# Head-slot DMAs moved from SyncE to GpSimd, with smaller gate/up weight buffers

## The chip, the cores and the metric

The kernel runs on one core of a Trainium2 chip. The metric is the device time of one launch in microseconds. The profile is one execution of the same program, recorded by the hardware profiler.

## The reference

Inputs are bf16: x [1, 2048, 576], wqkv [576, 1728], wo [576, 576], w_gate and w_up [576, 4608], w_down [4608, 576].

```python
def attention(xn):                      # 32 heads of 18, causal, window 256
    q, k, v = split_heads(xn @ wqkv)
    scores = (q @ k.T) * 18 ** -0.5
    p = softmax(where(0 <= i - j < 256, scores, -1e9))
    return merge_heads(p @ v) @ wo

def gated_ffn(xn):
    return (sigmoid(xn @ w_gate) * (xn @ w_up)) @ w_down

xn = layernorm(x)                       # no scale, no shift
out = x + attention(xn) * silu(gated_ffn(xn))
```

## The kernel before, in words

The 2048 rows are handled in four chunks of 512 (four blocks of 128). Each chunk goes through these steps: the layer norm (`build_ln`, L359), which leaves the transposed chunk in `xnT` (TensorE transposes at L394); the V projection (L469, L472); the q/k projection (`build_qk`, L408); attention for eight head groups of four heads (`build_attn`, L494); the output projection (`build_wo`, L593); and the FFN (`build_ffn`, L644). The FFN's first product makes gate and up for 36 tiles of 128 columns (L687, and L697 for the last 64 rows of the contraction). Its second product contracts over these 36 tiles (L743, L745).

**The head slots.** The q/k projection makes 1152 columns in nine tiles of 128, two tiles to a group, so five groups. VectorE copies a group from PSUM to `qd` (L430). A head has 18 columns, and the score product wants each head at a partition that is a multiple of 32, so for each head's q and each head's k one DMA inside SBUF moves its 18 rows of 512 bf16 elements into its slot in `qT` or `kT`. A head that straddles two tiles takes two DMAs. That gives 72 DMAs per chunk and 288 in all: 16 in each of the first four groups, 8 in the fifth. A head group's score products (L523) wait for all slot DMAs of the groups that hold its columns: head group 0 needs group 0, head group 1 needs groups 0 and 1, head group 7 needs groups 3 and 4. `qd` has two buffers, `qT` has four.

**The weights.** The gate/up weights are read from HBM again in every chunk, because SBUF doesn't hold them. `wgs` has two buffers, each for four of the 36 tiles; `weights(fg)` (L659) fills one with four DMAs: 512 rows of gate, 64 rows of gate, the same for up. A row of such a transfer is 512 columns, 1024 bytes. A buffer is released by the last product of its four tiles. `w_down` is loaded once, during chunk 0, and stays.

**What sets the order.** Every instruction is an `Op` with an engine, an estimated duration, what it depends on and a priority (0 goes first). `schedule` (L779) simulates the five engines with these estimates and takes, for each engine in turn, the operation with the smallest (start + 150 ns x priority). What comes out is one fixed list per engine, and each engine works through its list in order; nothing is reordered on the chip. All DMAs are issued by SyncE: `dma` (L187) makes an `Op` on "SP" of 620 ns, with 2000 ns to landing and 280 bytes per ns for all of them together. Loads of x have priority 0, slot DMAs 1, `wqkv` and stores 2, gate/up weights 3, `w_down` and the second read of x 6. Compute on the attention side has priority 1, on the FFN side 3, so the FFN fills the gaps of attention.

A DMA carries a semaphore of its own lane, which counts 16 when the transfer has landed; `emit` (L851) puts the waits ahead of the instruction that needs them. GpSimd ("POOL") has only the constants at the start (L316 to L332) and one small operation per block in the layer norm, the power that makes `rstd` (L377). VectorE's next step of the norm (L381) waits for it.

Of the kernel before, what the change touches and what calls it, by code (L numbers as in the profile page):

```python
# [18 lines left out]
BPC = NT // P  # L19
FG = 4  # L20
NFG = NFT // FG
EPS = 1e-5
SM_SCALE = float(DH) ** -0.5

# [9 lines left out]
NFIN = 2  # L34
NQK = 5

DMA_ISSUE_NS = 620.0
DMA_LAT_NS = 2000.0
DMA_BYTES_PER_NS = 280.0

# [118 lines left out]
class Builder:  # L159
# [24 lines left out]
            d.succs.append(o)  # L184
        return o

    def dma(self, dst, src, nbytes, name, lane, deps=(), prio=2):  # L187
        o = self.op("SP", DMA_ISSUE_NS, lambda eng: eng.dma_start(dst, src), name, deps, prio, nbytes=nbytes)  # L188
        o.lane = self.lane_ids.setdefault(lane, len(self.lane_ids))
        return o  # L190

    def alloc_memory(self):
        nc = self.nc
        bf16, f32 = dt.bfloat16, dt.float32
        cur = [(nc.sbuf_base + 63) // 64 * 64]
        top = nc.sbuf_top

        def size(shape, dtp):
            n = 1
            for s_ in shape[1:]:  # L200
                n *= s_
            return n * mybir.dt.size(dtp)

        def seq(name, shape, dtp=bf16):
            off = cur[0]
            cur[0] = (off + size(shape, dtp) + 31) // 32 * 32
            assert cur[0] <= top, f"out of SBUF at {name}: {cur[0]} > {top}"
            return nc.alloc_sbuf_tensor_at(name, list(shape), dtp, offset=off), off

        self.xnT, _ = seq("xnT", [P, 2, KT, NT])  # L210
        self.wd_sb, _ = seq("wd_sb", [P, NFT, D])
        self.hT, _ = seq("hT", [P, NFT, NT])
        self.wgs, _ = seq("wgs", [P, 2, 9, FG * P])
        self.tring, _ = seq("tring", [P, 2, NT])
        self.v_aug, _ = seq("v_aug", [P, NVB, H, DH + 1])
        self.qT, _ = seq("qT", [P, NQS, NT])
        self.kT, _ = seq("kT", [P, 2, NHG, NT])
        self.expr, zex = seq("expr", [P, NEX, 4, NT])
        self.stage = nc.alloc_sbuf_tensor_at("stage", [P, KT, 2 * D], bf16, offset=zex)
        assert size([P, KT, 2 * D], bf16) <= size([P, NEX, 4, NT], bf16)  # L220
        self.o_tok, _ = seq("o_tok", [P, BPC * D + 64])
        self.oT, _ = seq("oT", [P, 2, KT, P])
        self.s_attn, _ = seq("s_attn", [P, 2 * BPC, D])
        self.wqk, _ = seq("wqk", [P, KT, 2 * D])
        self.wv_sb, _ = seq("wv_sb", [P, KT, D])
        self.wo_sb, _ = seq("wo_sb", [P, KT, D])
        self.qd, _ = seq("qd", [P, NQD, 2, NT])
        self.xr, _ = seq("xr", [P, NXR, D])
        self.xnr, _ = seq("xnr", [P, NXN, KT * P])
        self.xf, _ = seq("xf", [P, NFIN, D])  # L230
        self.thf, _ = seq("thf", [P, NFIN, D])
        self.ident, _ = seq("ident", [P, P])
        self.mask, _ = seq("mask", [P, 4, P])
        self.neghalf, _ = seq("neghalf", [P, 1], f32)
        self.bnst, _ = seq("bnst", [P, NST, 2, 6], f32)
        self.mv, _ = seq("mv", [P, NST, 2], f32)
        self.veps, _ = seq("veps", [P, NST, 1], f32)
        self.rstd, _ = seq("rstd", [P, NST, 1], f32)
        self.rrec, _ = seq("rrec", [P, 2, 4 * BPC], f32)
        if self.verbose:  # L240
            print(f"SBUF used up to {cur[0]} of {top} ({top - cur[0]} free)")
        self.ps = nc.alloc_psum_tensor("ps", [P, 4096], f32)
        self.psb = self.ps.bitcast(bf16)
        self.pool_s = Pool("S", [0, 1])
        self.pool_f = Pool("F", [2, 3])

    def build_graph(self):
        self.r_xr = Ring(NXR, "xr")
        self.r_xn = Ring(NXN, "xnr")
        self.r_st = Ring(NST, "stats")  # L250
        self.r_qd = Ring(NQD, "qd")
        self.r_q = Ring(NQS, "q")
        self.r_ex = Ring(NEX, "expr")
        self.r_rec = Ring(2, "rrec")
        self.r_oT = Ring(2, "oT")
        self.r_w = Ring(2, "wgs")
        self.r_t = Ring(2, "tring")
        self.r_xf = Ring(NFIN, "xf")
        self.r_th = Ring(NFIN, "th")
        self.xnT_rel = [[] for _ in range(NC)]  # L260
        self.op_xnT = [[] for _ in range(NC)]
        self.op_v = {}
        self.op_vis = {}
        self.last_vis = None
        self.ffn_last = None
        self.op_pv = {}
        self.op_on = {}
        self.op_s = {}
        self.op_q2 = {}
        self.otr_last = []  # L270
        self.prev_f2_last = None
        self.x_dma = {}
        self.q_slot = {}
        self.op_sp = {}
        self.sp_grp = {}
        self.hg_grps = {}

        self.load_x(0)
        self.build_consts()
        for c in range(NC):  # L280
            self.build_ln(c)
            self.build_v(c)
            made = 0
            for hg in range(NHG):
                need = min(NQK, (8 * UNIT * (hg + 2) - 1) // (2 * P) + 1)
                while made < need:
                    self.build_qk(c, made)
                    made += 1
                self.build_attn(c, hg)
            self.build_wo(c)  # L290
            self.build_ffn(c)
# [116 lines left out]
    def build_qk(self, c, gi):  # L408
# [25 lines left out]
        for j in range(NUNIT):  # L434
            hg, w, h4 = j // 8, (j % 8) // 4, j % 4
            for i, t in enumerate(ts):
# [9 lines left out]
                else:  # L446
# [1 line left out]
                    dst = self.kT[p0:p0 + hi - lo, par, hg, :]  # L448
                src = self.qd[lo - t * P:hi - t * P, sq, i, :]
                o = self.dma(dst, src, (hi - lo) * NT * 2, f"dma:sp:{c}:{j}:{t}", ("qk", par, gi),  # L450
                             deps=[ev, war], prio=1)
                self.op_sp.setdefault((c, hg), []).append(o)
                self.sp_grp.setdefault((c, gi), []).append(o)
                self.r_qd.release(sq, o)
# [189 lines left out]
    def build_ffn(self, c):  # L644
# [11 lines left out]
            self.ffn_last = o  # L656
            return o

        def weights(fg):  # L659
            sw, dw = self.r_w.produce()  # L660
            fc = slice(fg * FG * P, (fg + 1) * FG * P)
            ds = []
            for w, (src, nm) in enumerate(((self.wg, "g"), (self.wu, "u"))):
                ds.append(self.dma(self.wgs[:, sw, 4 * w:4 * w + 4, :],
                                   src[0:512, fc].rearrange("(kt p) f -> p kt f", p=P), 512 * 512 * 2,
                                   f"dma:w{nm}:{c}:{fg}", ("w", sw, w), deps=[dw], prio=3))
                ds.append(self.dma(self.wgs[64 * w:64 * w + 64, sw, 8, :], src[512:576, fc], 64 * 512 * 2,
                                   f"dma:w{nm}4:{c}:{fg}", ("w", sw, 2 + w), deps=[dw], prio=3))
            slots[fg] = sw
            wops[fg] = ds  # L670
            if c == 0:
                self.op_wd.append(self.dma(
                    self.wd_sb[:, fg * FG:(fg + 1) * FG, :],
                    self.wd[fg * 512:(fg + 1) * 512, :].rearrange("(kt p) d -> p kt d", p=P), 512 * D * 2,
                    f"dma:wd{fg}", ("wd", fg), deps=[hm.get(fg * FG - FG)], prio=6))

        def bank(h, w):
            o = h.units[0] * 1024 + 512 * w
            return self.ps[:, o:o + 512]

        def main(ft, h, w, first, acq):
            sw, fc = slots[ft // FG], slice((ft % FG) * P, (ft % FG + 1) * P)

            def f(eng):
                res = None
# [1 line left out]
                    res = eng.matmul(bank(h, w), self.wgs[:, sw, 4 * w + kt, fc], x_in[:, kt, :],  # L687
                                     start=(first and kt == 0), stop=(not first and kt == 3))
                return res
            return pe(4 * mm_ns(NT), f, f"f1{'gu'[w]}:{c}:{ft}", [self.op_xnT[c], wops[ft // FG]], acq)  # L690

        def rem(eng, ft, h, first):
            sw, fc = slots[ft // FG], slice((ft % FG) * P, (ft % FG + 1) * P)
            res = None
            for w in range(2):
                r = slice(64 * w, 64 * w + 64)
                res = eng.matmul(bank(h, w), self.wgs[r, sw, 8, fc], x_in[r, 4, :], start=first, stop=not first,  # L697
                                 tile_position=(64 * w, 0))
            return res
# [12 lines left out]

        for fa in range(0, NFT, 2):
            fb = fa + 1
            if fa % FG == 0:
                weights(fa // FG)
            ha, hb = self.pool_f.hold(), self.pool_f.hold()
            main(fa, ha, 0, True, ha)
            main(fa, ha, 1, True, None)
# [6 lines left out]
            g = main(fb, hb, 0, False, None)  # L726
            u = main(fb, hb, 1, False, None)
            tail(fb, hb, g, u)
            if fb % FG == FG - 1:
                self.r_w.release(slots[fb // FG], u)  # L730
        self.xnT_rel[c].append(self.ffn_last)

        new_last = [None] * NFG
# [45 lines left out]
    def schedule(self):  # L779
# [13 lines left out]
        while nsched < len(ops):  # L793
# [32 lines left out]
            if o.acq is not None:  # L826
                o.deps += [d for d in o.acq.pool.take(o.acq, units) if d not in o.deps]
            o.start = stt
            if o.eng == "SP":
                free["SP"] = stt + o.est  # L830
                o.end = max(stt + o.est + DMA_LAT_NS, bw_clock + o.nbytes / DMA_BYTES_PER_NS)
                bw_clock = max(bw_clock, stt + o.est) + o.nbytes / DMA_BYTES_PER_NS
            else:
# [17 lines left out]
    def emit(self):  # L851
        nc = self.nc
        ENGS = ("PE", "ACT", "DVE", "POOL", "SP")
        for o in self.ops:
            if o.eng == "SP":
                o.needs_tok = True
            for d in o.deps:
                d.needs_tok = True
# [3 lines left out]
        for e in ENGS:  # L862
            for o in self.prog[e]:
                if not o.needs_tok:
                    continue
                if e == "SP":
                    lane_cnt[o.lane] += 16
                    o.tok = (("L", o.lane), lane_cnt[o.lane])
                else:
# [6 lines left out]
        def run_engine(e, eng):  # L876
            known = {}
            for o in self.prog[e]:
# [9 lines left out]
                    eng.wait_ge(semof(k), v)  # L888
                ins = o.fn(eng)
                if o.needs_tok:  # L890
                    ins.then_inc(semof(o.tok[0]), 16 if e == "SP" else 1)
            if e == "SP":
                for i, n in enumerate(lane_cnt):
                    if n > 0:
# [65 lines left out]
```

## Time and profile before

| what | us |
|---|---|
| median of 3 runs | 690.53 |
| lowest and highest run | 689.25, 694.64 |
| the profiled execution | 692.99 |
| its span, first to last instruction | 691.3 |
| mean granted TensorE clock in it | 0.958 of 2.4 GHz |

The rows below are from the profiled execution. Engines are PE (TensorE's matmuls), PEld (its weight loads), DVE (VectorE), ACT (ScalarE), POOL (GpSimd) and SP (SyncE). A name with q behind it, as SPq, is the engine's queue of instructions; a DMA is issued there, and its issue doesn't count as busy time. L188 is the line in `dma` that issues every DMA. A tile is named as the program names it: `wgs<-in_B_w_up_dram` is a load of up weights, `qT<-qd` a slot DMA. Times are in us from the start of the span, unless a column says ns.

### The profile page before, as it was taken

The page shows a single profiled execution, that of the slowest core. Times are in us where ns is not written, and L with a number is a line of the kernel's source. Part 1 is how long each engine was busy: PE and PEld are TensorE (multiplying, and loading weights), DVE is VectorE, ACT ScalarE, POOL GpSimd, SP SyncE. Part 2 cuts the span into 40 slices and gives each one's busy share as a digit, 9 for nine tenths or more (in the row PEclk, how much of TensorE's full clock was granted, in tenths as well). Part 3 has the DMA queues.
Part 4 walks back from the last instruction along what each step waited for, and adds up shares of the span by engine and source line. Part 5 has one row for each costly group of instructions (what it writes and reads, how often), then busy time and mean ns, then how long its engine had stood idle before and what let it go on. Part 6 is the DMA issues. An engine that isn't in the chain of part 4 may idle for free.

```text
span 691.3 us, 13052 instructions
## 1 busy us (share of the span) xinstructions
PE 615.9 (89%) x5555; PEld 288.5 (42%) x5652; DVE 284.3 (41%) x493; ACT 290.4 (42%) x302; POOL 15.5 (2%) x32
## 2 busy tenths in 40 slices
PE   3997796999889999579959999997899999999996
PEld 1442242444445444224425554443344454333453
DVE  3664353534544643333534324555352222333222
ACT  3444444636446642355656314756452101322200
POOL 4110000000000000000000000000000000000000
PEclk9999898999999999789989999999899999999999
DMA  9515626415011320144052001233323311555000
GB/s 286 167 40 160 199 81 183 141 52 164 11 31 45 95 70 13 51 123 134 15 149 70 19 14 53 86 89 90 120 86 85 123 35 54 155 155 151 2 29 23
DMA packets 64425, 63.08 MB, mean 91 GB/s; under 512 B 5808, under 2 KB 63792, under 8 KB 64368
## 3 DMA queue, kind: packets, MB, share of 16 engines
q1 hardware_dynamic: 64368, 62.25, 30.1%
q8 instruction: 44, 0.72, 0.4%
q14 instruction: 13, 0.11, 0.1%
HBM read 55.15 MB, written 2.36 MB: 83 GB/s over the span
## 4 chain that ended last, share of the span: by engine, by line
PE 72%; SPq 11%; DMA 6%; DVE 4%; issue 3%; ACT 3%; DVEq 0%; ACTq 0%
PE ps L687 32%; PE ps L743 15%; SPq L188 11%; PE ps L564 5%; PE ps L697 4%; PE ps L421 4%; PE ps L523 3%; PE ps L745 3%; DMA wgs<-in_B_w_up_dram 3%; PE ps L627 3%; PE ps L469 2%; ACT expr L539 2%; DMA xr<-in_A_x_dram 1%; DMA wv_sb<-in_A_wqkv_dram 1%; DVE hT L706 1%
## 5 line engine op out<-in xcount | busy, mean ns | idle before, releaser
L687 PE MATMUL ps<-xnT,wgs 128*128 128x512 bf16 x1102 | 276.1, 391 | 31.5 <-DMA wgs<-in_B_w_up_dram 20.4
L539 ACT ACTIVATE expr<-ps 128x2048 bf16<-128x2048 f32 (+1 forms) x96 | 170.0, 1771 | 121.0 <-PE ps L523 120.6
L687 PEld LDWEIGHTS ps<-xnT,wgs 128*128 128x128 bf16 x1152 | 103.2, 99 | 168.7 <-issue 65.2
L743 PE MATMUL ps<-wd_sb,hT 128*128 128x512 bf16 x543 | 143.9, 385 | 0.0
L703 ACT ACTIVATE tring<-ps 128x512 bf16<-128x512 f32 x144 | 84.6, 597 | 139.0 <-PE ps L697 119.0
L547 DVE TENSOR_TENSOR expr<-expr,mask 128x1536 bf16<-128x1536 bf16 (+2 forms) x96 | 78.9, 824 | 150.7 <-ACT expr L539 150.7
L706 DVE SCALAR_TENSOR_TENSOR hT<-tring,ps 128x512 bf16<-128x512 bf16 x144 | 97.6, 685 | 102.4 <-ACT tring L703 70.0
L745 PE MATMUL ps<-wd_sb,hT 128*128 128x64 bf16 x576 | 111.7, 194 | 2.3 <-issue 0.7
L743 PEld LDWEIGHTS ps<-wd_sb,hT 128*128 128x128 bf16 x576 | 56.8, 99 | 69.0 <-issue 5.5
L745 PEld LDWEIGHTS ps<-wd_sb,hT 128*128 128x128 bf16 x576 | 56.8, 99 | 0.5
L523 PE MATMUL ps<-qT,kT 18*128 18x256 bf16 (+1 forms) x960 | 38.1, 251 | 16.0 <-ACT expr L539 8.7
L564 PEld LDWEIGHTS ps<-v_aug,expr 128*128 128x128 bf16 x1440 | 40.5, 96 | 13.3 <-DVE expr L547 4.9
L697 PE MATMUL ps<-xnT,wgs 64*128 64x512 bf16 x288 | 45.7, 398 | 0.0
L421 PE MATMUL ps<-xnT,wqk 128*128 128x512 bf16 x175 | 43.0, 392 | 2.6 <-ACT expr L539 2.4
L564 PE MATMUL ps<-v_aug,expr 128*128 128x19 bf16 x1440 | 41.2, 172 | 4.6 <-DVE expr L547 2.3
L766 ACT ACTIVATE thf<-ps 128x576 bf16<-128x576 f32 x16 | 10.4, 649 | 75.1 <-PE ps L745 75.0
L523 PEld LDWEIGHTS ps<-qT,kT 18*128 18x128 bf16 x960 | 15.9, 93 | 55.8 <-ACT expr L539 21.5
L768 DVE SCALAR_TENSOR_TENSOR thf<-thf,ps 128x576 bf16<-128x576 bf16 x16 | 12.0, 752 | 61.5 <-ACT thf L766 61.5
L430 DVE CAST qd<-ps 128x1024 bf16<-128x1024 f32 (+1 forms) x20 | 22.3, 1117 | 28.1 <-PE ps L421 28.1
L421 PEld LDWEIGHTS ps<-xnT,wqk 128*128 128x128 bf16 x180 | 17.4, 100 | 24.3 <-ACT expr L539 3.6
L469 PE MATMUL ps<-wv_sb,xnT 128*128 128x512 bf16 x73 | 20.3, 406 | 3.1 <-DMA wv_sb<-in_A_wqkv_dram 2.3
L638 ACT ACTIVATE s_attn<-ps 128x576 bf16<-128x576 f32 x16 | 10.4, 650 | 23.3 <-PE ps L630 23.3
(44 smaller groups left out, 209.8 us busy)
## 6 DMA issues: line engine op xcount, KB each, us to landing
wgs<-in_B_w_gate_dram SPq DMA_DIRECT2D x36, 512.0 KB, 4.2
wgs<-in_B_w_up_dram SPq DMA_DIRECT2D x36, 512.0 KB, 5.3
wd_sb<-in_B_w_down_dram SPq DMA_DIRECT2D x9, 576.0 KB, 5.9
wgs<-in_B_w_gate_dram SPq DMA_DIRECT2D x36, 64.0 KB, 4.0
wgs<-in_B_w_up_dram SPq DMA_DIRECT2D x36, 64.0 KB, 4.9
xf<-in_A_x_dram SPq DMA_DIRECT2D x16, 144.0 KB, 2.1
out_dram<-xf SPq DMA_DIRECT2D x16, 144.0 KB, 1.9
qT<-qd SPq DMA_DIRECT2D x112, 18.0 KB
```

What stands on the lines that cost most here:

```text
L188: o = self.op("SP", DMA_ISSUE_NS, lambda eng: eng.dma_start(dst, src), name, deps, prio, nbytes=nbytes)
L421: res = eng.matmul(self.ps[:, b + i * 512:b + (i + 1) * 512], self.wqk[:, kt, t * P:(t + 1) * P], self.xnT[:, xs, kt, :], start=(kt == 0), ...
L523: res = eng.matmul(self.ps[:, o:o + nq * P], self.kT[r, kp, hg, ko:ko + P], self.qT[r, qs, q0 * P:(q0 + nq) * P], start=True, stop=True, t ...
L539: return eng.activation(dst, src, ACTF.Exp, scale=SM_SCALE)
L547: return eng.tensor_tensor(e_, e_, m_, ALU.mult)
L564: res = eng.matmul(self.ps[:, o:o + 19], self.expr[:, se, h4, at * P:(at + 1) * P], self.v_aug[:, kb % NVB, hg * 4 + h4, :], start=(n == 0 ...
L687: res = eng.matmul(bank(h, w), self.wgs[:, sw, 4 * w + kt, fc], x_in[:, kt, :], start=(first and kt == 0), stop=(not first and kt == 3))
L697: res = eng.matmul(bank(h, w), self.wgs[r, sw, 8, fc], x_in[r, 4, :], start=first, stop=not first, tile_position=(64 * w, 0))
L703: th = op("ACT", act_ns(NT), lambda e: e.activation(self.tring[:, st, :], bank(h, 0), ACTF.Tanh, scale=0.5), f"th:{c}:{ft}", deps=[pg, dt_ ...
L706: mu = op("DVE", dve_ns(NT), lambda e: e.scalar_tensor_tensor(self.hT[:, ft, :], self.tring[:, st, :], 1.0, bank(h, 1), ALU.add, ALU.mult) ...
L743: eng.matmul(self.ps[:, b:b + 512], self.hT[:, ft, cols], self.wd_sb[:, ft, 0:512], start=(ft == 0), stop=(ft == NFT - 1))
L745: res = eng.matmul(self.ps[:, b + 512:b + 576], self.hT[:, ft, cols], self.wd_sb[:, ft, 512:576], start=(ft == 0), stop=(ft == NFT - 1))
```

## The change

Slot DMAs are issued from GpSimd's queue, and the planner counts 1000 ns for each there; a DMA on SP counts 600 ns. `wgs` has four buffers of two tiles, in the same memory, so a transfer's row is 256 columns (512 bytes), and each chunk has 18 loads of four DMAs. The first such load of chunk 0 has priority 1, all others 3 as before. `w_down` keeps its loads of four tiles. The rest of the diff lets the planner and `emit` treat a DMA by its lane and not by its engine.

```diff
+WG = 2
+NWS = 4
-DMA_ISSUE_NS = 620.0
+DMA_ISSUE_NS = {"SP": 600.0, "POOL": 1000.0}
...
-    def dma(self, dst, src, nbytes, name, lane, deps=(), prio=2):
-        o = self.op("SP", DMA_ISSUE_NS, lambda eng: eng.dma_start(dst, src), name, deps, prio, nbytes=nbytes)
+    def dma(self, dst, src, nbytes, name, lane, deps=(), prio=2, eng="SP"):
+        o = self.op(eng, DMA_ISSUE_NS[eng], lambda e: e.dma_start(dst, src), name, deps, prio, nbytes=nbytes)
...
-        self.wgs, _ = seq("wgs", [P, 2, 9, FG * P])
+        self.wgs, _ = seq("wgs", [P, NWS, 9, WG * P])
...
-        self.r_w = Ring(2, "wgs")
+        self.r_w = Ring(NWS, "wgs")
...
                 o = self.dma(dst, src, (hi - lo) * NT * 2, f"dma:sp:{c}:{j}:{t}", ("qk", par, gi),
-                             deps=[ev, war], prio=1)
+                             deps=[ev, war], prio=1, eng="POOL")
...
-        def weights(fg):
+        def weights(wg):
             sw, dw = self.r_w.produce()
-            fc = slice(fg * FG * P, (fg + 1) * FG * P)
+            pr = 3 if c or wg else 1
+            fc = slice(wg * WG * P, (wg + 1) * WG * P)
...
-            if fa % FG == 0:
-                weights(fa // FG)
+            if fa % WG == 0:
+                weights(fa // WG)
+            if c == 0 and fa % FG == 0:
+                load_wd(fa // FG)
...
-            if fb % FG == FG - 1:
-                self.r_w.release(slots[fb // FG], u)
+            if fb % WG == WG - 1:
+                self.r_w.release(slots[fb // WG], u)
...
-            if o.eng == "SP":
-                free["SP"] = stt + o.est
+            if o.lane is not None:
+                free[o.eng] = stt + o.est
```

## Rows read from the trace of the kernel before

**Rows 1.** The page, busy time, share of the span and instructions of each engine.

```profile
PE 615.9 (89%) x5555; PEld 288.5 (42%) x5652; DVE 284.3 (41%) x493; ACT 290.4 (42%) x302; POOL 15.5 (2%) x32
```

**Rows 2.** The page, shares of the span in the chain that ended last, by engine.

```profile
PE 72%; SPq 11%; DMA 6%; DVE 4%; issue 3%; ACT 3%; DVEq 0%; ACTq 0%
```

**Rows 3.** The waits of engines and of SP's queue: total us, times, longest us.

```profile
PE ps L687 <- DMA wgs<-in_B_w_up_dram: 20.4, 6, 3.8
...
DVE bnst L369 <- DMA xr<-in_A_x_dram: 13.2, 5, 7.5
...
SPq L188 <- DVE xf L774: 94.9, 10, 25.8
```

**Rows 4.** SP's queue in time, start of chunk 2: start us, us, instruction, count.

```profile
266.60 3.05 SPq L188 DMA_DIRECT2D qT<-qd  x4
...
289.90 0.66 SPq L188 DMA_DIRECT2D kT<-qd  x1
290.60 1.03 SPq L188 DMA_DIRECT2D wgs<-in_B_w_gate_dram  x2
```

**Rows 5.** TensorE in time; in brackets its idle time before, and what ended it.

```profile
13.71 2.29 PE L469 MATMUL ps<-wv_sb,xnT 128*128 128x512 bf16 x5 [2.33 <-DMA wv_sb<-in_A_wqkv_dram]
...
287.84 3.90 PE L421 MATMUL ps<-xnT,wqk 128*128 128x512 bf16 x9 [2.38 <-ACT expr L539]
...
297.70 3.19 PE L687 MATMUL ps<-xnT,wgs 128*128 128x512 bf16 x7 [3.43 <-DMA wgs<-in_B_w_up_dram]
```

**Rows 6.** The chain that ended last, in order of time: start us, us, what.

```profile
192.80 2.65 DMA qT<-qd
...
290.56 0.04 issue
...
292.31 4.88 DMA wgs<-in_B_w_up_dram
...
415.10 1.75 DMA kT<-qd
```

**Rows 7.** Stretches: from:to, length, busy time of each engine, PEclk, DMA share, GB/s.

```profile
0.00:13.70 13.70, 1.98 (x15) 1.37 (x16) 5.87 (x25) 5.27 (x6) 8.08 (x20) 1.00 0.88 275
53.00:82.00 29.00, 21.30 (x179) 7.97 (x182) 10.19 (x17) 12.97 (x14) 0.00 (x0) 0.82 0.63 191
104.00:125.00 21.00, 14.84 (x131) 5.76 (x135) 7.70 (x14) 10.73 (x12) 0.00 (x0) 0.84 0.58 177
162.00:200.00 38.00, 33.36 (x405) 17.88 (x412) 19.00 (x42) 16.61 (x13) 2.29 (x3) 0.91 0.29 85
277.00:318.00 41.00, 27.02 (x266) 11.20 (x269) 14.07 (x20) 19.31 (x17) 0.00 (x0) 0.75 0.35 101
347.00:365.00 18.00, 10.84 (x129) 4.52 (x129) 6.26 (x9) 9.79 (x8) 0.00 (x0) 0.81 0.47 141
474.00:490.00 16.00, 11.23 (x81) 3.90 (x81) 5.08 (x8) 8.10 (x6) 0.00 (x0) 0.79 0.54 159
365.00:474.00 109.00, 105.97 (x1148) 54.04 (x1165) 49.77 (x78) 54.62 (x50) 0.00 (x0) 1.00 0.18 54
577.00:651.00 74.00, 73.63 (x357) 28.86 (x363) 26.43 (x39) 21.95 (x37) 0.00 (x0) 1.00 0.39 116
```

**Rows 8.** Instructions of line 188: count, issue time ns min/median/max, first and last start us.

```profile
L188 SPq DMA_DIRECT2D qT<-qd x144: 560/698/945, 26.0 to 478.2; - x144
L188 SPq DMA_DIRECT2D kT<-qd x144: 557/698/798, 29.2 to 481.1; - x144
L188 SPq DMA_DIRECT2D wgs<-in_B_w_gate_dram x72: 367/517/1971, 5.1 to 634.6; - x72
```

**Rows 9.** Groups of instructions by line: busy us, mean ns | idle before, releaser.

```profile
L377 POOL TENSOR_TENSOR rstd<-veps,neghalf 128x1 f32<-128x1 f32 x16 | 9.6, 607 | 161.0 <-DVE veps L375 161.0
...
L547 DVE TENSOR_TENSOR expr<-expr,mask 128x1536 bf16<-128x1536 bf16 (+2 forms) x96 | 78.9, 824 | 150.7 <-ACT expr L539 150.7
...
L381 DVE TENSOR_SCALAR xnr<-xr,mv,rstd 128x576 bf16<-128x576 bf16 x16 | 6.5, 425 | 3.6 <-POOL rstd L377 3.3 <-PE ps L394 0.3
```

More of the change, by code (lines that the diff above doesn't have):

```diff
@@ L664, in weights, with load_wd @@
                 ds.append(self.dma(self.wgs[:, sw, 4 * w:4 * w + 4, :],
[L665 to L675, printed above, removed]
+                                   src[0:512, fc].rearrange("(kt p) f -> p kt f", p=P), 512 * WG * P * 2,
+                                   f"dma:w{nm}:{c}:{wg}", ("w", sw, w), deps=[dw], prio=pr))
+                ds.append(self.dma(self.wgs[64 * w:64 * w + 64, sw, 8, :], src[512:576, fc], 64 * WG * P * 2,
+                                   f"dma:w{nm}4:{c}:{wg}", ("w", sw, 2 + w), deps=[dw], prio=pr))
+            slots[wg] = sw
+            wops[wg] = ds
+        def load_wd(fg):
+            self.op_wd.append(self.dma(
+                self.wd_sb[:, fg * FG:(fg + 1) * FG, :],
+                self.wd[fg * 512:(fg + 1) * 512, :].rearrange("(kt p) d -> p kt d", p=P), 512 * D * 2,
+                f"dma:wd{fg}", ("wd", fg), deps=[hm.get(fg * FG - FG)], prio=6))
         def bank(h, w):
@@ L681, in main @@
         def main(ft, h, w, first, acq):
-            sw, fc = slots[ft // FG], slice((ft % FG) * P, (ft % FG + 1) * P)
+            sw, fc = slots[ft // WG], slice((ft % WG) * P, (ft % WG + 1) * P)
             def f(eng):
@@ L689, in f @@
                 return res
-            return pe(4 * mm_ns(NT), f, f"f1{'gu'[w]}:{c}:{ft}", [self.op_xnT[c], wops[ft // FG]], acq)
+            return pe(4 * mm_ns(NT), f, f"f1{'gu'[w]}:{c}:{ft}", [self.op_xnT[c], wops[ft // WG]], acq)
         def rem(eng, ft, h, first):
-            sw, fc = slots[ft // FG], slice((ft % FG) * P, (ft % FG + 1) * P)
+            sw, fc = slots[ft // WG], slice((ft % WG) * P, (ft % WG + 1) * P)
             res = None
@@ L854, in emit @@
         for o in self.ops:
-            if o.eng == "SP":
+            if o.lane is not None:
                 o.needs_tok = True
@@ L865, in emit @@
                     continue
-                if e == "SP":
+                if o.lane is not None:
                     lane_cnt[o.lane] += 16
@@ L890, in run_engine @@
                 if o.needs_tok:
-                    ins.then_inc(semof(o.tok[0]), 16 if e == "SP" else 1)
+                    ins.then_inc(semof(o.tok[0]), 16 if o.lane is not None else 1)
             if e == "SP":
```

## The prediction

> **What bounds the kernel now.** I read the page's busy line, its chain, the list of waits, then the SP queue and TensorE side by side in time, and last a table of stretches. TensorE is busy for 615.9 of 691.3 us [rows 1]: it is the bound, and what can be won is its idle time and its time at the lower clock. The chain that ended last is 72% TensorE, but 11% (some 78 us) of it is SP's queue issuing DMAs and 6% is DMA [rows 2]. The waits say what TensorE misses: six stalls on gate/up weights, 20.4 us in all; VectorE loses 13.2 us to late loads of x, 7.5 of them in one wait that a mask multiplication stands behind [rows 3].
>
> Why are weights late? SP's own time line shows it [rows 4]. From 266.60 to 290.56 us SP issues 32 head-slot transfers for chunk 2, the first two of its five groups: 23.96 us, 0.75 us each. The weights that chunk 2's FFN wants are issued behind them, at 290.60. TensorE meanwhile first waits for exponentials with nothing else in its list (2.38 us before 287.84), then 3.43 us for those weights [rows 5], and the chain of that stretch runs along the slot issues into the weight transfer, which takes 4.88 us from 292.31 [rows 6]. The program's order is fixed beforehand by a planner that counts 0.62 us per DMA; 32 of them at 0.75 are 4.1 us late, which is about the size of the stalls. Behind a stall the granted clock is at 1.2 instead of 2.4 GHz for some microseconds (a mean of 0.75 in 277 to 318 [rows 7]).
>
> What these stretches cost: length minus busy time times granted clock is what full-speed work would have left over. For the first six stretches of [rows 7] after the opening one that is 29.0 - 21.30 x 0.82 = 11.5; 21.0 - 14.84 x 0.84 = 8.5; 38.0 - 33.36 x 0.91 = 7.6; 41.0 - 27.02 x 0.75 = 20.7; 18.0 - 10.84 x 0.81 = 9.2; 16.0 - 11.23 x 0.79 = 7.1: together 65 us of 163. An undisturbed stretch of the same mixed work, 365 to 474, loses 3.03 of 109, or 2.8% [rows 7]; 163 us at that rate are 4.5. So 60 us hang on what SP issues late.
>
> **The change part by part.** *Slot DMAs to GpSimd.* All 288 (144 to each of two tiles [rows 8]) leave SP: 288 x 0.75 = 216 us of issue time. Weights and x loads are no longer queued behind them, and the planner knows it, so FFN work can stand where 277 to 290 had none. I credit the whole 60 us, including 162 to 200, where the late transfer is x.
>
> What it adds is 288 issues on POOL's queue. No row shows a DMA issued there. From below the nearest is SP's own issue of the same transfer, median 0.70 us, with its gap of 0.04 some 0.74; from above the longest issue of a weight DMA on SP, 1.97 us [rows 6, 8]. POOL's one repeated small operation takes 0.607 us, nearly all fixed cost [rows 9]; adding it to 0.74 gives 1.35. I take 1.05, halfway from 0.74 to 1.35, nearest to SP's row for the same transfer. The planner now counts 1.00 and fills that time with FFN work, so not the whole of it costs, only what reality adds to 1.00. The lateness can pile up over the first two groups of a chunk, 32 DMAs, because head groups 0 and 1 wait for them; later groups run ahead, since eight head groups use five groups of transfers. Four chunks make 128 DMAs: 128 x 0.05 = 6 us. The ends: at 1.97, 128 x 0.97 = 124 us; at 0.70, 128 x 0.30 = 38 us gained at most, of which I credit nothing, since an early landing doesn't move an instruction forward in a fixed list.
>
> Landing: on SP a slot transfer ends 1.75 to 2.65 us after its issue in the chain's waits [rows 6]. For POOL's no row exists: from nothing to 1 us more (half such a landing) at 8 places (two groups, four chunks), 0 to 8 us; I take 4. A landing sooner by the same would be hidden by the fixed order.
>
> Queued behind slot DMAs on POOL now: the 16 small rstd operations of the layer norm [rows 9], for which VectorE and then the transposes wait. A slot DMA waits for VectorE's cast or for a head group to give its slot free, and an rstd behind it waits along. The 12 of the later chunks meet at most one issue each if the planner places them as it believes, 12 x 1.05 = 13 us of VectorE; it is busy for 284.3 us of 691.3 [rows 1], which is the cover: 0. Without it, those 13 us.
>
> A rule against this part: the Trainium skill, "DMA: Bandwidth & Descriptors", section "Issuing engines are not separate DMA queues", says that issuing from several engines only saves issue time on the sequencer, usually small beside the transfer. By it the 60 us would be 0 and the time that of rival 3. Here the chain has SP's issue in it [rows 2, 6], and a slot transfer is at most 18 rows of 1 KB.
>
> *Four buffers of two tiles.* Same bytes, 144 weight DMAs become 288. At a median of 0.517 us plus a gap of 0.04 [rows 6, 8] that adds 144 x 0.56 = 80 us to SP, against 216 taken away: hidden. Rows of a transfer shrink from 1024 to 512 bytes. DMA share in the pure FFN stretch is 0.39 [rows 7]: at the same time per byte it stays, at the same time per packet it doubles to 0.78. Both are under 1, and a buffer is freed twice as often with three others in reserve: 0. Only a share over 1 would uncover it, and then each per cent over costs 0.74 us of such a 74 us stretch.
>
> *Weights first at the start.* TensorE's first long work waited 2.33 us until 13.71 for the V weights [rows 5]. Gate/up weights now land earlier, but FFN work needs all four transposed blocks of x. Bounds: 2.3 us gained if they are used in this gap; against it 0.6 MB moved ahead of the V weights at the 275 GB/s of the opening [rows 7] is 2.1 us lost. I take 0.
>
> **Sum**, from the profiled execution's 692.99 us (1.7 outside its span): 692.99 - 60 + 6 + 4 + 0 = 643. The median of the runs is 690.53, 2.5 lower: **641 us**. No order can beat TensorE's own work: 615.9 less 20 at half speed (busy times lost clock over the six stretches) plus the 11.7 idle of the opening [rows 1, 7], about 607.
>
> **The rivals.**
> *1. GpSimd issues too slowly (slower).* Each slot DMA holds POOL for much over its planned 1.00 us, and in-order TensorE stands before head groups 0 and 1 of each chunk instead of before weights. Price 128 x (t - 1.00) against 56 won: it decides from t = 1.44 us. At the upper row, 1.97, the time is 692.99 - 60 + 124 + 4 - 2.5 = 758. For it: planned and real SP times differ already. Against it: the transfer needs 0.70 elsewhere, and POOL's small operation 0.607.
> *2. VectorE holds POOL up.* Each mask multiplication (96 of 0.824 us, 78.9 in all [rows 9]) keeps one POOL issue waiting to its end. In the gated share, 32 of 72 per chunk, that is 78.9 x 32 / 72 = 35 us: 676. Against it: the multiplications take two inputs from SBUF, and no row shows the two engines together. Beside it: the Trainium skill, "SBUF — State Buffer", section "SBUF: two separate sides", warns that a VectorE operation in a two-port mode locks GpSimd out and starves the descriptors of its DMAs. No run here shows that yet; by the page two-input operations lock only against GpSimd reads, which would leave the smaller normalisations (16 of 0.425 us [rows 9]).
> *3. Nothing won.* SP stays an in-order queue: weights now stand behind a store that waits for the final sum; SP waited 94.9 us for such sums [rows 3]. If weights come late there, the idle time moves: 690. Against it: those waits lie where the second FFN product keeps TensorE full.
>
> **How the numbers follow.** Forecast 0.70 (618 to 662 by its own terms: background losses better filled, or t near 1.2); rival 2 0.12; rival 3 0.08; rival 1 0.10. Faster by over 1% is the forecast and rival 2: 0.82. Within 1% (what a measurement of this kernel can hardly tell from no change) 0.08; slower 0.10. The range runs from 618, and to 685 so that it takes in rival 2 and a t of 1.33; rivals 1 and 3 are left out.
>
> **What would show it right or wrong.** Right: no TensorE wait on gate/up weights longer than 1 us, the 7.5 us wait for x gone, SP's share of the chain near nothing, granted clock 1.00 through what were the six stretches. POOL's issue rows decide the rest: about 1.05 us each, the scores' waits for slot tiles below some 15 us. Wrong: issues above 1.4 us with long waits of the scores on the slot tiles at each chunk's start (rival 1); long POOL issues only beside mask multiplications (rival 2); weight waits that go on under another releaser (rival 3).

## The result, and the profile after

The changed kernel takes 636.17 us (median of 4 runs, 635.73 to 636.56), the kernel before 689.89 beside it: a ratio of 0.9212, 95% interval 0.9164 to 0.9259. A second measurement later gave 635.81 and 0.9208 (0.9182 to 0.9234). The profiled execution took 635.73 us with a span of 634.0, so 57.3 less than the profiled execution before.

The page of the changed kernel: busy time by engine, then the shares in the chain by engine. They answer to [rows 1, 2].

```profile
PE 606.4 (96%) x5652; PEld 285.0 (45%) x5652; DVE 284.6 (45%) x493; ACT 290.8 (46%) x302; POOL 160.2 (25%) x320
...
PE 90%; ACT 3%; DVE 3%; issue 2%; DMA 1%; SPq 1%; DVEq 0%
```

SP's queue has gone from 11% of the chain to 1%, and TensorE from 72% to 90%. POOL's 160.2 us contain its 288 DMA issues, 145.8 us, which the page counts as busy on that engine. TensorE's busy times of the two pages can't be subtracted as they stand: this page has a record of all 5652 products, the page before of 5555, and a missing record takes busy time with it. The same kernel profiled again (e12 below, span 634.0 us) has 5559:

```profile
PE 598.5 (94%) x5559; PEld 285.1 (45%) x5652; DVE 284.4 (45%) x493; ACT 290.5 (46%) x302; POOL 159.6 (25%) x320
```

Beside it the kernel before has 17.4 us more of busy time and 39.9 us more of idle time. The work that ran at 1.2 GHz now runs at 2.4 GHz (a mean granted clock of 1.0 against 0.958).

The waits, where [rows 3] had 20.4 us of TensorE for weights and 13.2 us of VectorE for x. No row of TensorE waiting for weights or slot tiles is left. VectorE's wait for x, and TensorE's largest one inside the FFN behind the opening:

```profile
DVE bnst L371 <- DMA xr<-in_A_x_dram: 7.1, 3, 4.3
...
PE ps L691 <- DVE hT L710: 4.5, 5, 1.0
```

POOL's queue and then SP's at the start of chunk 2 (start us, us, instruction, count), where [rows 4] showed 32 slot issues on SP with the weights behind them.

```profile
265.98 2.00 POOL L190 DMA_DIRECT2D qT<-qd  x4 [37.74 <-DVE o_tok L589]
...
272.51 1.50 POOL L190 DMA_DIRECT2D kT<-qd  x3
280.77 1.03 POOL L190 DMA_DIRECT2D kT<-qd  x2 [6.75 <-DVE hT L710]
...
288.30 0.51 POOL L190 DMA_DIRECT2D kT<-qd  x1
```

```profile
267.92 0.94 SPq L190 DMA_DIRECT2D wgs<-in_B_w_gate_dram  x2
268.89 1.16 SPq L190 DMA_DIRECT2D wgs<-in_B_w_up_dram  x2
281.14 0.94 SPq L190 DMA_DIRECT2D wgs<-in_B_w_gate_dram  x2
```

The weights of the same microseconds go out on SP while POOL issues slots, and no weight stands behind a slot. A slot DMA holds POOL for half a microsecond. The instructions of the issuing line (count, ns min/median/max) answer to [rows 8]:

```profile
L190 SPq DMA_DIRECT2D wgs<-in_B_w_gate_dram x144: 367/516/1875, 2.6 to 577.3; - x144
...
L190 POOL DMA_DIRECT2D qT<-qd x144: 505/508/728, 33.1 to 466.6; - x144
L190 POOL DMA_DIRECT2D kT<-qd x144: 505/507/554, 35.3 to 468.6; - x144
```

Stretches of the changed kernel (length, busy time of PE, PEld, DVE, ACT, POOL, then PEclk, DMA share, GB/s), against [rows 7]:

```profile
40.00:120.00 80.00, 78.74 (x656) 32.82 (x652) 37.70 (x60) 40.64 (x48) 33.35 (x67) 1.00 0.63 177
120.00:260.00 140.00, 134.38 (x1461) 65.52 (x1449) 70.25 (x121) 76.17 (x71) 38.39 (x75) 1.00 0.28 77
260.00:500.00 240.00, 237.03 (x2523) 115.50 (x2522) 113.38 (x172) 129.69 (x118) 72.41 (x144) 1.00 0.29 80
...
520.00:588.00 68.00, 68.00 (x334) 26.38 (x333) 24.02 (x36) 19.91 (x34) 0.00 (x0) 1.00 0.45 126
```

From 40 to 500 us TensorE is idle for 9.9 us of 460, and the granted clock reads 1.00 in all three stretches; before, six stretches of 163 us in all lost 65 us in idle time and lower clock.

### The profile page after: what moved, and what is told of

It reads as the page before. It is cut to its first block, busy times and chain, and to the rows that moved or that the text cites. A ratio compares the mean times of both kernels' runs of the same rounds, so it can differ in the third digit from the quotient of the medians.

```text
span 634.0 us, 13361 instructions
## 1 busy us (share of the span) xinstructions
PE 606.4 (96%) x5652; PEld 285.0 (45%) x5652; DVE 284.6 (45%) x493; ACT 290.8 (46%) x302; POOL 160.2 (25%) x320
## 4 chain that ended last, share of the span: by engine, by line
PE 90%; ACT 3%; DVE 3%; issue 2%; DMA 1%; SPq 1%; DVEq 0%
PE ps L691 39%; PE ps L749 20%; PE ps L423 6%; PE ps L566 5%; PE ps L701 5%; PE ps L525 5%; PE ps L471 3%; ACT expr L541 3%; PE ps L629 3%; PE ps L751 3%; DMA stage<-in_A_wqkv_dram 1%; DVE qd L432 1%; PE ps L607 1%; PE ps L396 1%; DVE hT L710 1%
## 5 line engine op out<-in xcount | busy, mean ns | idle before, releaser
L691 PE MATMUL ps<-xnT,wgs 128*128 128x512 bf16 x1152 | 273.2, 381 | 6.6 <-DVE hT L710 4.5
L691 PEld LDWEIGHTS ps<-xnT,wgs 128*128 128x128 bf16 x1152 | 101.7, 98 | 145.1 <-issue 38.7
L749 PE MATMUL ps<-wd_sb,hT 128*128 128x512 bf16 x576 | 149.1, 380 | 0.0
L549 DVE TENSOR_TENSOR expr<-expr,mask 128x1536 bf16<-128x1536 bf16 (+2 forms) x96 | 79.2, 825 | 129.2 <-ACT expr L541 129.1
L190 POOL DMA_DIRECT2D qT<-qd x144 | 73.1, 514 | 213.5 <-DVE rrec L581 109.3
L190 POOL DMA_DIRECT2D kT<-qd x144 | 72.7, 511 | 52.7 <-DVE rrec L581 18.7
L701 PE MATMUL ps<-xnT,wgs 64*128 64x512 bf16 x288 | 43.6, 381 | 0.3 <-DVE thf L774 0.3
```

The lines of the kernel that those rows point to most:

```text
L190: o = self.op(eng, DMA_ISSUE_NS[eng], lambda e: e.dma_start(dst, src), name, deps, prio, nbytes=nbytes)
L549: return eng.tensor_tensor(e_, e_, m_, ALU.mult)
L749: eng.matmul(self.ps[:, b:b + 512], self.hT[:, ft, cols], self.wd_sb[:, ft, 0:512], start=(ft == 0), stop=(ft == NFT - 1))
```

## The experiments

Three theories. **A**: weights and x came late because they stood behind slot DMAs on SP; **B**: the smaller and more numerous weight buffers made the gain; **C**: the plan's wrong issue time for SP (0.62 us where 0.75 were needed) made the loss. Each was tried by a part of the change alone.

**Slot DMAs on POOL alone** (e1): the changed kernel with the old weight buffers and no early load.

```diff
-WG = 2
-NWS = 4
+WG = 4
+NWS = 2
...
-            pr = 3 if c or wg else 1
+            pr = 3
```

> Slot DMAs on POOL (planned at 1.00 us), but the weights as before: two buffers of four tiles, no early first load. Theory A (the loss came from weights and x queued behind slot DMAs on SP): nearly the whole gain, 636 to 646 us, no TensorE wait on weights over 1 us. Theory B (the four smaller buffers, refilled earlier, made the gain): above 665 us, waits on weights remain.

633.05 us, ratio 0.9164 (0.9127 to 0.9201), and one TensorE wait on weights in the list, 0.2 us long. The move to POOL alone brings the whole gain.

**The weight buffers and the early load alone** (e2): the changed kernel with the slot DMAs back on SP.

```diff
-                             deps=[ev, war], prio=1, eng="POOL")
+                             deps=[ev, war], prio=1)
...
-DMA_ISSUE_NS = {"SP": 600.0, "POOL": 1000.0}
+DMA_ISSUE_NS = {"SP": 620.0, "POOL": 1000.0}
```

> Four buffers of two tiles and the early first load, but slot DMAs stay on SP, all DMAs planned at 620 ns. Theory A: no gain or a loss, 685 to 710 us, because SP issues 144 more DMAs through the same queue and the plan is still 0.13 us short for each of 288 slot DMAs. Theory B: below 660 us.

685.39 us, ratio 0.9932 (0.9901 to 0.9962): 0.7% faster, and TensorE's waits on weights (total us, times, longest) stay. B falls.

```profile
PE ps L691 <- DMA wgs<-in_B_w_up_dram: 15.2, 6, 3.7
```

**An honest plan on SP** (e3), made from the kernel before.

```diff
-    def dma(self, dst, src, nbytes, name, lane, deps=(), prio=2):
-        o = self.op("SP", DMA_ISSUE_NS, lambda eng: eng.dma_start(dst, src), name, deps, prio, nbytes=nbytes)
+    def dma(self, dst, src, nbytes, name, lane, deps=(), prio=2, est=DMA_ISSUE_NS):
+        o = self.op("SP", est, lambda eng: eng.dma_start(dst, src), name, deps, prio, nbytes=nbytes)
...
-                             deps=[ev, war], prio=1)
+                             deps=[ev, war], prio=1, est=750.0)
```

> The kernel before, with one number changed: the planner counts 750 ns for a slot DMA on SP, as measured, in place of 620. Theory C (the loss was a plan that did not know SP's issue time, and the queue itself has room): below 655 us. Theory A (SP has too much to issue at the start of a chunk whatever the plan knows): 665 to 685 us; the TensorE waits on weights shrink from 20.4 us to under 8, but waits on the exponentials take their place where the plan finds no FFN work.

692.39 us, ratio 1.0029 (1.0000 to 1.0059): nothing gained, so C falls. A's numbers were missed too: 665 to 685 us were expected, and weight waits under 8 us. Its TensorE waits, and below them the second one in the kernel before:

```profile
PE ps L687 <- DMA wgs<-in_B_w_up_dram: 19.7, 6, 5.2
PE ps L523 <- ACT expr L539: 16.9, 10, 2.0
```

```profile
PE ps L523 <- ACT expr L539: 8.7, 7, 2.0
```

Two of them in time, with the idle time before in brackets:

```profile
69.97 1.48 PE L687 MATMUL ps<-xnT,wgs 128*128 128x512 bf16 x3 [5.21 <-DMA wgs<-in_B_w_up_dram]
...
292.36 3.19 PE L687 MATMUL ps<-xnT,wgs 128*128 128x512 bf16 x7 [2.98 <-DMA wgs<-in_B_w_up_dram]
```

The waits on exponentials, 8.7 us before, grew to 16.9, as A expected, but beside the weight waits and not in their place. The slots still had priority over weights, so most weights still left after them, as SP's queue shows ahead of the second of these waits; a planner that knew how long that takes did not gain by it.

```profile
274.44 0.45 SPq L188 DMA_DIRECT2D wgs<-in_B_w_gate_dram  x1
274.93 3.00 SPq L188 DMA_DIRECT2D kT<-qd  x4
...
284.72 2.21 SPq L188 DMA_DIRECT2D qT<-qd  x3
286.97 0.54 SPq L188 DMA_DIRECT2D wgs<-in_B_w_gate_dram  x1
```

**Weights ahead of slots, all on SP** (e5): e3 and one more number.

```diff
-                                   f"dma:w{nm}:{c}:{fg}", ("w", sw, w), deps=[dw], prio=3))
+                                   f"dma:w{nm}:{c}:{fg}", ("w", sw, w), deps=[dw], prio=0))
...
-                                   f"dma:w{nm}4:{c}:{fg}", ("w", sw, 2 + w), deps=[dw], prio=3))
+                                   f"dma:w{nm}4:{c}:{fg}", ("w", sw, 2 + w), deps=[dw], prio=0))
```

> The kernel before with slot DMAs planned at 750 ns and the gate/up weights put ahead of slot DMAs in SP's order (priority 0 in place of 3). Theory A1 (only the order on SP was wrong: weights stood behind slots): below 655 us. Theory A2 (SP is one serial place: whichever goes first, the other waits): 675 to 700 us, the TensorE waits on weights nearly gone, and waits of the scores on slot tiles or of TensorE on exponentials in their place.

631.82 us, ratio 0.9138 (0.9102 to 0.9173). All 288 slot DMAs are on SP, at the same median of 0.70 us, the weights in two large buffers, and the gain is the same or a little more. SP's queue in this run:

```profile
263.19 2.92 SPq L188 DMA_DIRECT2D qT<-qd  x4
266.15 1.43 SPq L188 DMA_DIRECT2D kT<-qd  x2
267.63 1.03 SPq L188 DMA_DIRECT2D wgs<-in_B_w_gate_dram  x2
268.70 1.15 SPq L188 DMA_DIRECT2D wgs<-in_B_w_up_dram  x2
269.89 2.37 SPq L188 DMA_DIRECT2D kT<-qd  x3
```

Four weight issues (2.2 us) step in among the slots when a buffer is free, and no TensorE wait on weights is left. So A holds in its narrower form, A1: SP had room for everything, and its order, with up to 32 slot issues (24 us) ahead of four weight issues, made most of the loss. How much of it, the next run tells, since this one changed the plan's figure as well.

**The priority alone** (e9): the kernel before with e5's two edited lines and nothing else.

> The kernel before with one number changed: gate/up weights have priority 0 in place of 3, slot DMAs stay on SP and are planned at 620 ns. Theory A1 (the order on SP was the whole cause): within 3 us of the run that also had the measured 750 ns, 630 to 636 us. Rival (order and honest plan are both needed): 645 to 670 us, with waits of the scores on slot tiles, since the plan is 0.13 us short per slot DMA.

647.37 us, ratio 0.9394 (0.9352 to 0.9436): not A1's 630 to 636 us but inside the rival's range. No TensorE wait on weights is left; its waits on DMAs are for slot tiles:

```profile
PE ps L523 <- DMA kT<-qd: 8.3, 4, 2.8
...
PE ps L523 <- DMA qT<-qd: 2.8, 3, 1.3
```

Order alone brings some 41 us; the honest figure brings 16 more, but only once the order is right (e3). With the order right it is the scores, not the weights, that are late when the plan is short: 11.1 us here, 1.1 us in e5.

**The price of a POOL issue** (e7, e8). Each slot DMA is issued as two or three DMAs of part of the columns, with the plan and all engines' lists unchanged. One part takes POOL 0.505 us, as a whole one does.

```diff
+SPLIT = (0, 256, 512)                 # e8: (0, 176, 352, 512)
...
+            def f(e):
+                for a_, b_ in zip(SPLIT[:-2], SPLIT[1:-1]):
+                    e.dma_start(dst[:, a_:b_], src[:, a_:b_]).then_inc(self.lanes[o.lane], 16)
+                return e.dma_start(dst[:, SPLIT[-2]:], src[:, SPLIT[-2]:])
```

> The changed kernel with every slot DMA issued as two of half the columns, plan and every other list unchanged. One issue then holds POOL for about 1.02 us (2 x 0.51). By the prediction's price, 128 x 0.02 = 3 us over the changed kernel: 637 to 641 us. If each of the 288 counted beyond the measured 0.51, 288 x 0.51 = 147 us more: 780.

> The same with three parts, about 1.53 us of POOL per slot DMA, beyond the plan's 1.00. By the prediction's price 128 x 0.53 = 68 us: 704 us, slower than before, with the scores' waits on slot tiles at head groups 0 and 1 of each chunk. If later groups fall behind too, 288 x 0.53 = 153 us: 789. If FFN work in the list covers it all: below 645.

e7: 641.49 us (ratio 0.9264, 0.9215 to 0.9313), 5.7 over the changed kernel's 635.81. e8: 762.46 us (ratio 1.1025, 1.0979 to 1.1071), 126.7 over it. By the prediction's price they were to take 637 to 641 and 704 us; with every one of the 288 DMAs counting, e8 was to take 789. So rival 1 of the prediction is real, but POOL's issue of 0.51 us is far from where it decides. The parts land no later than whole transfers (from issue to landing a median of 1.9 us in e8 and 2.2 in the changed kernel), so it is POOL's time that costs. TensorE's waits in e8, and the four waits of its chunk 2:

```profile
PE ps L534 <- DMA kT<-qd: 55.6, 8, 8.6
PE ps L534 <- DMA qT<-qd: 41.8, 8, 7.7
```

```profile
358.40 0.61 PE L534 MATMUL ps<-qT,kT 18*128 18x256 bf16 x12 [7.83 <-DMA kT<-qd]
...
382.29 0.61 PE L534 MATMUL ps<-qT,kT 18*128 18x256 bf16 x12 [6.59 <-DMA kT<-qd]
...
407.88 0.40 PE L534 MATMUL ps<-qT,kT 18*128 18x256 bf16 x12 [1.22 <-DMA qT<-qd]
...
446.27 0.61 PE L534 MATMUL ps<-qT,kT 18*128 18x256 bf16 x12 [7.34 <-DMA qT<-qd]
```

There are 16 such waits, 97.4 us, four in each chunk and not two. In chunk 2 they stand before head groups 0, 1, 3 and 5, the first that need slot groups 0, 1, 2 and 3: all four groups of 16 come late, and only the fifth, of 8, doesn't. The other 29 us go with work at the lower clock (a mean granted clock of 0.931; TensorE's busy time is 628.5 us in e8 and 598.5 in e12, with 5559 records in both). Over the 0.515 us by which 1.515 exceeds the plan, 126.7 us are what 246 DMAs would cost, not 128; four groups of 16 in four chunks are 256.

**The plan told POOL's real time** (e6).

```diff
-DMA_ISSUE_NS = {"SP": 600.0, "POOL": 1000.0}
+DMA_ISSUE_NS = {"SP": 600.0, "POOL": 510.0}
```

> The changed kernel, with the planner told the measured 510 ns for a slot DMA on POOL in place of 1000. Theory D (the plan's surplus of 0.49 us per DMA costs nothing, because FFN work fills it): 634 to 638 us. Rival (attention is planned too late, and the end moves with it): 626 to 632 us.

635.22 us, ratio 0.9187 (0.9148 to 0.9226): no difference that can be measured, as D expected. A plan that counts too much costs nothing here; one that counts too little did (e8, and e9 beside e5).

**The opening** (e4, e12, e11, e10). e4 is the changed kernel with `pr = 3` for all weights; e12 is the changed kernel again.

> The changed kernel without the early first load (priority 3 for all weights). If the early load is worth what the opening suggests (first FFN product at 14.89 us, V weights late), 1 to 2 us slower than the changed kernel, 637 to 638 us; if FFN work at the opening only takes the place of the V projection, 636 us.

> The changed kernel once more, in more rounds, to place it against the run without the early first load (ratio 0.9156). If the early load costs the 2 to 4 us that the opening of the traces suggests: a ratio of 0.919 to 0.923, 635 to 637 us. If the difference was the chip: 0.914 to 0.917.

e4: 632.29 us, ratio 0.9156 (0.9127 to 0.9185); e12: 635.81, ratio 0.9208 (0.9182 to 0.9234). The early load costs some 3.6 us (633.02 is the longest run without it, 634.87 the shortest with it); neither of the times expected for e4 (637 to 638, or 636 us) came. TensorE's opening in the changed kernel, and then in e4:

```profile
14.89 1.89 PE L691 MATMUL ps<-xnT,wgs 128*128 128x512 bf16 x4 [2.06 <-ACT xnT L405]
16.57 2.34 PE L471 MATMUL ps<-wv_sb,xnT 128*128 128x512 bf16 x5
```

```profile
12.98 2.29 PE L471 MATMUL ps<-wv_sb,xnT 128*128 128x512 bf16 x5 [1.55 <-DMA wv_sb<-in_A_wqkv_dram]
```

With the early load the first long work starts 1.9 us later, and the V projection 3.6 us later. From 300 us to the end the two traces run 3.1 us apart, so the loss lies ahead of that; how it adds up between the opening and there was not followed. FFN work needs all four transposed blocks; V needs one. The chain of the changed kernel's opening (start us, us, what) runs through the q/k weights, now landing later, and ScalarE's pack of them, which stands ahead of the copy of the last transposed block:

```profile
4.89 8.17 DMA stage<-in_A_wqkv_dram
13.08 0.58 ACT wqk L358
14.15 0.70 ACT xnT L405
14.89 1.89 PE ps L691 x4
```

Loading gate/up weights first need not cost anything in itself: e5 issues two loads of them ahead of all of `wqkv`, and takes 631.82 us. There the q/k weights are issued only at 9.44 us, the copy of the last transposed block starts at 12.82 us with no pack ahead of it, and the first FFN product at 13.58.

e11 is e4 with the V weights' two DMAs at priority 1.

> The changed kernel without the early gate/up load and with the V weights loaded ahead of the q/k weights. TensorE's wait of 1.55 us on V weights should go, some of the half-clock work with it: 630 to 631 us against 632.3 for the same without this. If the q/k weights then come late for the pack, 632 to 634 us.

631.67 us, ratio 0.9175 (0.9142 to 0.9207): the wait of 1.55 us is gone, but the 630 to 631 us expected did not come, and no gain over e4 can be told.

e10 is e5 with priority 3 for the first load alone.

> Slot DMAs on SP planned at 750 ns, weights ahead of slots, but the very first weight load back behind the weights of the V projection (priority 3), as in the changed kernel without its early load. If the early load costs the same 4 us here: 628 us. If the opening of this order hides it (its first FFN product came after 0.8 us of waiting): 631 to 632 us.

643.20 us, ratio 0.9347 (0.9314 to 0.9380): slower than e5 by 11 us, where 628 or 631 to 632 were expected. It doesn't answer its question, because the second load, still at priority 0, went ahead of the V weights:

```profile
17.44 2.29 PE L469 MATMUL ps<-wv_sb,xnT 128*128 128x512 bf16 x5 [4.66 <-DMA wv_sb<-in_A_wqkv_dram]
```

The opening shows about 4 us of the 11 (e5's first long work starts at 13.58); where the planner's other choices lost the rest was not settled.

e1, e4, e5 and e11 lie at 631.7 to 633.1 us: all a little below the changed kernel, and with each other the same.

## Why the prediction was right, and where its steps failed

641 us were predicted, 636.2 measured; the direction, the size and the place were right. Point by point:

*The stretches.* 60 us were to come back. Without the early load the span went from 691.3 to 630.8, so 60.5; the table of stretches gave the size of the gain well. It gave the parts as well: of its 65 us, 44 are idle time, 40 without what undisturbed work loses, and 20 are lower clock; measured are 39.9 us of idle time and 17.4 us of busy time. The signs named for it came: no weight wait, the longest wait for x 4.3 us in place of 7.5, SP out of the chain, full clock. One part isn't shown: 7.6 us in 162 to 200 were credited to late x, and e3, where no wait for x is longer than 2.5 us, gained nothing.

*Why weights were late.* The step "The program's order is fixed beforehand by a planner that counts 0.62 us per DMA; 32 of them at 0.75 are 4.1 us late, which is about the size of the stalls" failed as the cause of the stalls: e3 removed that error and the stalls stayed (19.7 us against 20.4), while e9 kept it and they went. The likeness of 4.1 and 3.4 us was chance. The main cause was priority, slots ahead of weights in one in-order queue, worth some 41 us by itself; the planner's error was worth some 16 us more, and only behind the right order. With that, "moved off SP" was enough but not needed, as e5 shows.

*The slot DMA on POOL.* 1.05 us were taken, 0.70 was the lower end; it is 0.508, below both. The 6 us fall away. The lower bound was wrong in kind: SP's time for a transfer bounds nothing on another engine's queue. The term's other factor, 128 DMAs that can be late because "later groups run ahead", was mis-sized too: 246 by e8, where the third and fourth groups came late as well. It also left out the lower clock behind a stall, 29 of e8's 126.7 us, which the prediction does count for the weights. At such a price and 55 us to lose, a slot DMA would decide from 1.00 + 55 / 246 = 1.22 us (an estimate, on a straight line from the plan's 1.00 to e8), not from 1.44.

*Landing.* 4 us were put in. The page shows 2.2 us (q) and 2.5 us (k) from issue to landing on POOL, and the scores wait for no slot tile: 0.

*The rstd operations.* Costed at 0 under VectorE's cover. VectorE waits 3.9 us for them, 3.3 before, so the 0 held.

*The four buffers.* Costed at 0: e1 with two buffers and e4 with four are the same within their intervals. The 512-byte rows took 0.45 of the DMA engines at 126 GB/s against 0.39 at 116, 6% more per byte, near the lower of the two bounds.

*Weights first.* Costed at 0 between a gain of 2.3 and a loss of 2.1; it loses about 3.6. The step left out that x's last transposed block is also copied by ScalarE, behind the pack of q/k weights: the first FFN product waits for that copy.

*Rival 2* (VectorE holds POOL up) is excluded here for the mask multiplications, 79.2 us in all: 37 of the 288 issues overlap one of them in the trace, and none of these took longer than 0.517 us, the median 0.507. That agrees with the Trainium skill, "SBUF — State Buffer", section "SBUF: two separate sides", in that two-input operations lock only against GpSimd reads. The longest issue of all, 0.728 us, is the only one beside a normalisation; a single case decides nothing about those. *Rival 3*: SP waits longer for the final sums than before (190.0 us against 94.9), but not where TensorE needs weights.

So the sum came out 5 us too high by errors of both signs. Between the profiled executions it is 7.3 us too high (643 against 635.73): 10 us of POOL costs that don't exist, less 3.2 for an opening that costs, and 0.5 of the stretches. The 2.5 us taken off from profiled execution to median brought it nearer by luck, since the changed kernel's profiled execution lies below its median.

## What to carry to other kernels

When an in-order DMA queue shows in the chain, ask first who stands behind whom: a few bulk loads that the bound engine needs belong ahead of a long run of small ones, and one priority with an honest issue time can be worth as much as a second queue. Give the planner the measured issue time, and rather too much than too little: the surplus was free, the deficit came straight out of the bound engine, with the lower clock on top. With the order wrong, the right figure alone gained nothing. At the opening, follow what the first possible product waits for: here it was not a weight but a copy that stood behind the pack of another load.

## What the hardware showed that was not expected

A DMA issued on POOL took 0.508 us where the same transfer took SP 0.698, and 0.505 us for a half or a third of the columns: a cost per DMA, not per byte, over these sizes. The Trainium skill, "DMA: Bandwidth & Descriptors", section "Issuing engine by pattern", calls the hardware path of the sync queue generally faster; for these transfers of at most 18 rows of 1 KB inside SBUF the time that a queue is held says the opposite. It says nothing of the landing: medians of 2.2 and 2.5 us on POOL, and 1.75 to 2.65 us in the chain's waits on SP [rows 6].
